# Fourier mixing and SoLU on one core: the first pair's x in 112 rows, F behind the first chunk, four more unread products

## The chip, the cores and the metric

The kernel runs on one core of one Trainium2 chip. The metric is the device time of one execution in microseconds. An execution of a kernel of this size differs from the next by some tenths of a microsecond. PE is TensorE (PEld its weight loads), DVE is VectorE, ACT is ScalarE, POOL is GpSimd and SP is SyncE, which here only issues transfers. TensorE's clock is granted in shares of its full speed.

## The reference

```python
X = np.fft.fft(x, axis=1)           # x: 8 x 3136 x 256, along the sequence
X = np.fft.fft(X, axis=2).real      # along the 256 features
x = X.reshape(25088, 256)
h = x @ w_in                        # w_in: 256 x 1024
e = np.exp(h - h.max(-1)); sm = e / e.sum(-1)
solu = h * sm
ln = (solu - mean(solu)) / sqrt(var(solu) + 1e-6) * g_ln
out = ln @ w_out                    # w_out: 1024 x 256
```

## The kernel before, in words

**Tiling.** The eight sequences are taken in four pairs. A sequence of 3136 is 49 x 64, so a pair has 2 x 49 = 98 rows (`PR`) of 64 positions with 256 features each. `load` (L119) brings a pair in eight chunks of four positions: `xa`, rows of 4 KB each, by a transfer that SP issues (L128), and the mirrored positions `xb` by an indirect transfer that POOL issues (L130, indices in `idx`). Chunk 7 also brings position 0 (L137). For the first pair each of these 16 transfers has 128 rows, though only 98 are used (L133); the 30 others are rows of the next sequence and nobody reads them. For the later pairs they have 98. Chunks 2 to 5 of the first pair land in the buffers called `room`.

**What is done with a chunk.** `add_mirror` (L146, L148) adds the mirrored half on DVE. `fold` (L153, L154, L166) then adds and subtracts the mirrored features into a tile `y`, which has two buffers. `transform1` multiplies with the table `F` on PE: chunks 0 and 2 straight from `xa` with `F` and its negative `minus` (L214), without a fold, the others from `y` (L225). ACT copies the result (L228), and `keep` (L233) stores it to `zd` in the chip's memory. After eight chunks `turn` (L241) reads `zd` back in another order, `transform2` (L253) makes a unit's `q`, and L289 multiplies with the weights: here the steady part begins, 100 units in which PE is nearly always busy. The first unit's first DVE instruction is L302.

**The weights in the opening.** The weights come as 64-bit numbers and are narrowed on DVE and ACT. `w_in` comes in four pieces of 512 KB (L591); piece 0 and 1 make the two halves of `w_in[0]`, 2 and 3 those of `w_in[1]` (`narrow_in`, which ends with L644). The feature transform is put into the weights: `product_in` (L698) multiplies the table `Q` with `w_in`. Its parts are numbered; parts 0 and 2 read `w_in[0]`, parts 1 and 3 read `w_in[1]`. `scale_out` (L722) transposes the gains `gain` on PE, and ACT copies them (L723). `w_out` follows as `raw_out` (L717).

**The order is written by hand.** Nothing is reordered: each engine takes its instructions in the order of the program. For PE in the opening that is: eight unread products (`busy`, L703, with a zeroed table as the operand, which depend on nothing but that table), parts 0 and 2 of `product_in` for two halves of `Wi`, `scale_out`, part 1 for both halves, then `transform1` chunk by chunk, with part 3 after chunks 0 and 3. For DVE: narrowing of the four pieces, with `add_mirror` of chunk 0 between the steps of the last one, then chunk after chunk. For SP: the pieces of `w_in` with `idx` and `Q` among them, `F`, `gain`, then `xa` of chunks 0 to 5; chunks 6 and 7 follow when chunks 0 and 1 are done. Transfers that SP issues use eight semaphores in turn, so the ninth waits until the first has landed, and so on.

Of the kernel before, what the change touches and what calls it, by code (L numbers as in the profile page):

```python
# [17 lines left out]
P = 128  # L18
# [5 lines left out]
PR = 2 * N1  # L24
# [21 lines left out]
def kernel(  # L46
# [19 lines left out]
    nc = tc.nc  # L66
# [23 lines left out]
    F = const.tile([PR, 6, ZR], FP32, name="F")  # L90

    T = [const.tile([P, 2, n, N2], FP32, name=f"T{n}") for n in (KG, NK - KG)]
# [4 lines left out]
    ident = const.tile([P, P], FP32, name="ident")  # L97
# [9 lines left out]
    def result(i):  # L107

        return banks[i % 4]
# [9 lines left out]
    def load(pr, c, room=None):  # L119

        r = slice(pr.p * PR, (pr.p + 1) * PR)
        rows = PR if pr.p else P
        if room is None:
            xa = xpool.tile([P, CH, D], FP32, tag="xa", name="xa")
            xb = xpool.tile([P, CH, D], FP32, tag="xb", name="xb")
        else:
            xa, xb = (t.rearrange("p (l d) -> p l d", d=D) for t in room)
        nc.sync.dma_start(out=xa[0:rows], in_=x_pn[r.start : r.start + rows, c * CH + 1 : (c + 1) * CH + 1, :])  # L128
        i = pr.p * NC + c
        nc.gpsimd.indirect_dma_start(  # L130
            out=xb[0:rows].rearrange("p l d -> p (l d)"), out_offset=None, in_=x_g,
            in_offset=bass.IndirectOffsetOnAxis(ap=idx[0:rows, i : i + 1], axis=0))
        xa, xb = xa[0:PR], xb[0:PR]  # L133
        x0 = None
        if c == NC - 1:
            x0 = xpool.tile([PR, 1, D], FP32, tag="x0", name="x0", bufs=1)
            nc.sync.dma_start(out=x0, in_=x_pn[r, 0:1, :])  # L137
        pr.raw[c] = (xa, xb, x0)
# [441 lines left out]
    NW = 512  # L580
# [66 lines left out]
    class Weights:  # L647
# [50 lines left out]
                nc.tensor.matmul(ps[:, fs], lhsT, self.w_in[c][:, fs], start=(c == 0), stop=(c == KD - 1))  # L698
            return ps

        def busy(self, i, n):
            for _ in range(n):
                nc.tensor.matmul(result(i)[:, 0 : NW // 2], ident, T[0].rearrange("p b k n -> p (b k n)")[:, 0 : NW // 2], start=True, stop=True)  # L703

        def keep_in(self, h, ps):
            nc.scalar.copy(w_mid if h == KD else Wi[:, h, :], ps)
# [62 lines left out]
    def ahead(pr, i, work, after=None):  # L769

        for c in range(NC):
            a = i - SUMS[pr.p][c]
            if work == "load" and (i == (pr.p - 1) * NK and c < 2 and (c or pr.p == 1) or a == 2 and c + 2 < NC):
                load(pr, c if a != 2 else c + 2)
            if work == "mirror" and a in (0, 1):
                behind(add_mirror(pr, c, nc.gpsimd, a), after or units[i - 1])
            if work == "fold" and a in (1, 2):
                fold_part(pr, c, a - 1)
# [24 lines left out]
    with tc.manual_schedule():  # L803
        pairs = [Pair(p) for p in range(NP)]
        first, weights = pairs[0], Weights()
# [13 lines left out]
        weights.piece_in(2)  # L819
        weights.load_tables()  # L820
        weights.piece_in(3)
        nc.sync.dma_start(out=F, in_=f_tab)
        weights.load_gain()
        for c in range(6):
            load(first, c, rooms.get(c))
        nc.vector.memset(ones, 1.0)
        nc.vector.memset(neg_half, -0.5)
        bits(top_bit, neg_half[:, 0:1].bitcast(I32), 31, ALU.logical_shift_right, 31, ALU.logical_shift_left)
# [10 lines left out]
        weights.mid()  # L839
        first.minus = fpool.tile([P, D], FP32, tag="ot1", name="minus", bufs=3)[0:PR, 0:ZR]  # L840
        nc.scalar.mul(out=first.minus, in_=F[:, 1, :], mul=-1.0)
        weights.busy(3, 8)
        made = [weights.product_in(h, (0, 2)) for h in range(KD)]
        weights.scale_out()
        for h in range(KD):
# [1 line left out]
        for c in range(NC):  # L847

            if c:
                add_mirror(first, c, nc.vector)  # L850
            if c not in BY_PE:
                fold(first, c)
            if c == NC - 1:
                for i in range(2):
                    weights.exponent_out(i)
                confine(weights.units[0], True)
                weights.narrow_out(0)
            if c == 3:
                weights.place_out()
                for i in range(2):  # L860
                    weights.load_out(i)
                weights.load_table(0)
            for s in range(CH // 2):
                if c == NC - 1:
                    confine(weights.units[0], parts=(s,))
                transform1(first, c * CH // 2 + s)
            first.raw.pop(c, None)
            if c + 6 < NC:
                load(first, c + 6)
            if c in (0, 3):  # L870
                weights.keep_in(c // 3, weights.product_in(c // 3, (3,), made[c // 3]))
# [310 lines left out]
```

## Time and profile before

| | |
|---|---|
| three executions | 1117.06, 1117.39 (median), 1117.9 us |
| the profiled execution's own time | 1116.79 us |
| its span | 1115.0 us, 22065 instructions |
| granted TensorE clock, mean over the span | 0.998 |
| DMA, mean | 168 GB/s, 187.76 MB |
| DMA in the first fortieth of the span | 338 GB/s, nine tenths busy or more |
| xa and room transfers of the first pair | 512 KB each, 4 + 4 |

How to read it: the span runs from the first to the last instruction of the profiled execution; the 1.8 us between it and the execution's own time lie before and after it. Times of instructions below count from the span's start. In a timeline a row gives start, length, engine, line, operation, output and inputs, shape and how often; brackets give the time for which the engine stood idle just before, and what ended it. Every fp32 matmul has two records, and every packet of a transfer of x is one row of 4096 bytes. A transfer is spread over up to 16 DMA engines, and each engine that takes part posts a share of its semaphore when its own rows have landed; the trace has the time of every such share.

### The profile page before, as it was taken

To read this page: it belongs to the slowest core of one execution; us is meant where nothing else is said; L and a number is where in the kernel's file an instruction comes from. 1 tells how busy PE (TensorE), PEld (TensorE's weight loads), DVE (VectorE), ACT (ScalarE), POOL (GpSimd) and SP (SyncE) were. 2 spreads that over 40 slices of the span, in tenths; PEclk is the share of its full clock that TensorE was granted. 3 is DMA by queue.
4 is the path that set the end of the run, shared out by engine and by line. 5 is a ranking of instruction groups with operands and counts; after the bars stand their busy time and mean duration, and the time that the engine had idled before them with its cause. 6 is when DMAs were issued, how large, how long until landed. Compare 5 with 4: busy or idle time off the path is not lost. (4 is left out here: it accounts for less than half of the span.)

```text
span 1115.0 us, 22065 instructions
## 1 busy us (share of the span) xinstructions
PE 1098.1 (98%) x7063; PEld 877.4 (79%) x7063; DVE 976.0 (88%) x1432; ACT 798.3 (72%) x1947; POOL 808.6 (73%) x709
## 2 busy tenths in 40 slices
PE   8899999999999999999999999999999999999998
PEld 5558787888887878788788778787887788778888
DVE  7998889898888988989889989898898898998884
ACT  5598777777767777777767777777776777777772
POOL 4168888867876979766878878885775676766665
PEclk9999999999999999999999999999999999999999
DMA  9655987757968979765898888776696785865665
GB/s 338 216 175 135 185 206 176 175 135 152 193 155 180 200 181 198 177 151 130 157 176 176 194 185 197 183 174 150 139 163 141 142 169 113 163 141 114 141 132 129
DMA packets 457930, 187.76 MB, mean 168 GB/s; under 512 B 424646, under 2 KB 439254, under 8 KB 457816
## 3 DMA queue, kind: packets, MB, share of 16 engines
q1 hardware_dynamic: 443800, 146.94, 62.1%
q0 software_dynamic: 14016, 39.40, 12.9%
q8 instruction: 58, 0.95, 0.4%
q14 instruction: 56, 0.46, 0.1%
HBM read 46.75 MB, written 38.80 MB: 77 GB/s over the span
## 5 line engine op out<-in xcount | busy, mean ns | idle before, releaser
L289 PE MATMUL ps_h<-Wi,q 128*128 128x512 f32 x800 | 361.6, 593 | 0.4 <-DVE nmax L310 0.2
L465 POOL TENSOR_TENSOR S<-uT 128x512 f32<-128x512 f32 x186 | 237.3, 1276 | 110.9 <-DVE u L325 35.9
L472 PE MATMUL ps_m<-Ws,S 128*128 128x128 f32 x2304 | 296.0, 275 | 0.0
L472 PEld LDWEIGHTS ps_m<-Ws,S 128*128 128x128 f32 x2304 | 279.5, 192 | 3.2 <-issue 0.2
L332 ACT ACTIVATE h<-u,usum 128x1024 f32<-128x1024 f32 x196 | 225.0, 1148 | 73.5 <-DVE u L325 67.3
L289 PEld LDWEIGHTS ps_h<-Wi,q 128*128 128x128 f32 x800 | 144.2, 190 | 144.9 <-issue 141.9
L325 DVE SCALAR_TENSOR_TENSOR u<-h,u 128x1024 f32<-128x1024 f32 x196 | 234.9, 1234 | 10.9 <-ACT u L318 10.8
L318 ACT ACTIVATE u<-h,nmax 128x1024 f32<-128x1024 f32 x196 | 223.3, 1141 | 2.4 <-DVE nmax L310 1.1
L396 DVE STREAM_TRANSPOSE v<-u 128x2048 f32<-128x2048 f32 x88 | 203.4, 2311 | 3.1
L472 PE MATMUL ps_m<-Wo,uT 128*128 128x128 f32 x1536 | 203.7, 276 | 0.0
L472 PEld LDWEIGHTS ps_m<-Wo,uT 128*128 128x128 f32 x1536 | 187.9, 192 | 1.0 <-issue 1.0
L310 DVE CUSTOM_DVE_ANT_0 h<-ev,ps_h 128x1024 f32<-128x1024 f32 x100 | 122.1, 1221 | 17.0 <-DVE ev L302 9.1
L310 DVE CUSTOM_DVE_ANT_0 h<-h,ps_h 128x1024 f32<-128x1024 f32 x96 | 117.2, 1221 | 14.2 <-ACT ot L516 0.5
L559 POOL DMA_INDIRECT out_dram<-ot,idx x96 | 109.0, 1135 | 27.0 <-issue 11.9
L465 POOL TENSOR_TENSOR S<-uT,S 128x512 f32<-128x512 f32 x93 | 118.8, 1277 | 7.2
L465 POOL TENSOR_TENSOR S<-S,uT 128x512 f32<-128x512 f32 x93 | 118.6, 1276 | 7.3
L302 DVE SCALAR_TENSOR_TENSOR ev<-w_mid,r,ps_h 128x1024 f32<-128x1024 f32 x99 | 122.8, 1241 | 0.3
L472 PE MATMUL ps_m<-Ws,uT 128*128 128x128 f32 x768 | 101.8, 276 | 0.0
L472 PE MATMUL ps_m<-Wo,S 128*128 128x128 f32 x768 | 101.4, 275 | 0.0
L253 PEld LDWEIGHTS ps_m<-T,g 128*128 128x128 f32 x400 | 60.0, 191 | 48.1 <-issue 45.9
L507 ACT ACTIVATE ot<-ps_m,rs 128x256 f32<-128x256 f32 x96 | 45.4, 473 | 71.0 <-PE ps_m L472 50.7
L472 PEld LDWEIGHTS ps_m<-Ws,uT 128*128 128x128 f32 x768 | 93.8, 192 | 0.0
(122 smaller groups left out, 1218.1 us busy)
## 6 DMA issues: line engine op xcount, KB each, us to landing
uT<-v SPq DMA_DIRECT2D x752, 128.0 KB
g<-zd POOLq DMA_DIRECT2D x72, 160.0 KB, 4.5
out_dram<-ot SPq DMA_DIRECT2D x176, 64.0 KB
zd<-z SPq DMA_DIRECT2D x24, 400.0 KB
xa<-in_x_dram SPq DMA_DIRECT2D x24, 392.0 KB
raw_in<-in_moe_w_in_dram SPq DMA_DIRECT2D x4, 512.0 KB
xa<-in_x_dram SPq DMA_DIRECT2D x4, 512.0 KB
room<-in_x_dram SPq DMA_DIRECT2D x4, 512.0 KB
```

Of the source, the lines that this page charges most:

```text
L253: nc.tensor.matmul(o, g[:, k, h * P : (h + 1) * P], table, start=(h == 0), stop=True, skip_group_check=True)
L289: nc.tensor.matmul(ps[:, fs], t.q[:, c * P : (c + 1) * P], Wi[:, c, fs], start=True, stop=not whole_even)
L302: nc.vector.scalar_tensor_tensor(out=t.ev, in0=w_mid, scalar=t.r, in1=ps, op0=ALU.mult, op1=ALU.add)
L310: nc.vector.tensor_tensor_reduce(out=t.h[s], in0=t.h[0] if s else t.ev, in1=t.odd, scale=1.0 if s else -0.5, scalar=3.0e38, op0=ALU.add, o ...
L318: nc.scalar.activation(out=t.u[s], in_=t.h[s], func=ACT.Exp, bias=t.nmax[:, s : s + 1], scale=-1.0, accum_out=t.esum[:, s : s + 1])
L325: t.last = nc.vector.scalar_tensor_tensor(out=t.u[s], in0=t.h[s], scalar=-1.0, in1=t.u[s], op0=ALU.mult, op1=ALU.mult, accum_out=t.usum[:, ...
L332: nc.scalar.activation(out=t.h[s], in_=t.u[s], func=ACT.Square, bias=t.usum[:, s : s + 1], scale=-float(FF), accum_out=t.ssq[:, s : s + 1])
L396: nc.vector.transpose(out=t.batch.v[:, :, t.w], in_=t.both.rearrange("p s (g n) -> p (s g) n", n=32))
L465: i = engine.tensor_tensor(out=S[j], in0=a, in1=b, op=op)
L472: nc.tensor.matmul(o, a[:, c], b[:, c], start=start and c == 0, stop=c == n - 1, skip_group_check=True)
L507: nc.scalar.mul(out=self.t.ot[1], in_=self.PP, mul=self.rs[1])
L559: dma = nc.gpsimd.indirect_dma_start(out=out, out_offset=bass.IndirectOffsetOnAxis(ap=idx[:, i : i + 1], axis=0), in_=t.ot[s], in_offset=None)
```

## The change

The 16 transfers of the first pair's x get 112 rows instead of 128. `F` and `gain` are issued after `xa` of chunk 0 instead of before it. `busy` gets its operand as an argument, and after the eight products on the zeroed table four more stand on the first 256 columns of `w_in[0]`; like the eight they write a bank that nobody reads. No other instruction is added or taken away, on no engine, and the order on the others stays.

```diff
@@ load
-        rows = PR if pr.p else P
+        rows = PR if pr.p else 112
@@ Weights
-        def busy(self, i, n):
+        def busy(self, i, n, rhs):
             for _ in range(n):
-                nc.tensor.matmul(result(i)[:, 0 : NW // 2], ident, T[0].rearrange("p b k n -> p (b k n)")[:, 0 : NW // 2], start=True, stop=True)
+                nc.tensor.matmul(result(i)[:, 0 : NW // 2], ident, rhs[:, 0 : NW // 2], start=True, stop=True)
@@ the opening
         weights.load_tables()
         weights.piece_in(3)
-        nc.sync.dma_start(out=F, in_=f_tab)
-        weights.load_gain()
         for c in range(6):
             load(first, c, rooms.get(c))
+            if c == 0:
+                nc.sync.dma_start(out=F, in_=f_tab)
+                weights.load_gain()
...
         nc.scalar.mul(out=first.minus, in_=F[:, 1, :], mul=-1.0)
-        weights.busy(3, 8)
+        weights.busy(3, 8, T[0].rearrange("p b k n -> p (b k n)"))
+        weights.busy(3, 4, weights.w_in[0])
         made = [weights.product_in(h, (0, 2)) for h in range(KD)]
         weights.scale_out()
         for h in range(KD):
             weights.product_in(h, (1,), made[h])
```

With this, SP's order is: the pieces with `idx` and `Q`, `xa` of chunk 0, `F`, `gain`, `xa` of chunk 1 and on. `gain` is now the ninth transfer and takes the wait for the first; `xa` of chunk 0 and `F` wait for none. On PE the first of the four new products waits for DVE's half of `w_in[0]`, and the first product on `Q` for `Q` alone.

## The prediction

> **What bounds the kernel now.** I read the page first: TensorE is busy in nearly the whole span, so a gain in the opening reaches the end only by starting the steady part earlier.
>
> ```profile
> PE 1098.1 (98%) x7063; PEld 877.4 (79%) x7063; DVE 976.0 (88%) x1432; ACT 798.3 (72%) x1947; POOL 808.6 (73%) x709
> ```
>
> The change touches the first 50 us alone. So I went to the table of stretches there (from:to, length, busy time and records of PE, PEld, DVE, ACT and POOL, granted clock, DMA share, GB/s).
>
> ```profile
> 8.22:11.63 3.41, 1.01 (x3) 0.52 (x4) 3.34 (x7) 2.49 (x5) 2.80 (x3) 1.00 1.03 344
> 11.63:15.04 3.41, 3.41 (x6) 1.35 (x5) 3.31 (x7) 2.73 (x5) 2.78 (x3) 0.50 1.02 352
> 18.00:32.20 14.20, 14.08 (x61) 9.98 (x60) 12.85 (x25) 7.11 (x12) 2.39 (x2) 1.00 1.03 410
> 22.00:32.00 10.00, 10.00 (x44) 7.01 (x42) 8.69 (x17) 6.35 (x10) 0.12 (x1) 1.00 1.02 411
> ```
>
> Two things bind from 18 to 32 us: the DMA engines are full at 410 GB/s, and PE has almost no gap. PE ran at half clock from 11.63 to 15.04, after a stretch with 1.01 of 3.41 us busy. Next the DVE timeline, whose brackets name the waits:
>
> ```profile
> 14.58 0.69 DVE L635 SCALAR_TENSOR_TENSOR raw_in<-raw_in,S 128x512 f32<-128x512 uint32 x1
> 16.77 1.22 DVE L146 TENSOR_TENSOR xa<-xa,xb 98x1020 f32<-98x1020 f32 x1 [1.50 <-DMA xa<-in_x_dram]
> ...
> 24.45 1.22 DVE L146 TENSOR_TENSOR room<-room 98x1020 f32<-98x1020 f32 x1 [1.26 <-DMA room<-in_x_dram]
> ...
> 32.86 1.22 DVE L146 TENSOR_TENSOR xa<-xa,xb 98x1020 f32<-98x1020 f32 x1 [0.58 <-DMA xa<-in_x_dram]
> ...
> 38.27 0.75 DVE L594 TENSOR_SCALAR S<-raw_out 128x512 int32<-128x512 int32 x2
> ```
>
> DVE waits for data three times, at chunks 0, 3 and 6, 3.34 us in all. From 32.86 on it works without a pause worth naming until L302 at 50.32, the first unit's start. This is the chain that sets when the steady part begins. PE's timeline shows the products that the change wants warm:
>
> ```profile
> 6.68 0.38 PE L703 MATMUL ps_m<-T,ident 128*128 128x256 f32 x1
> 10.62 5.37 PE L698 MATMUL wps<-w_in,Q 128*128 128x512 f32 x8 [3.56 <-DMA Q<-in_q_tab_dram]
> 15.92 0.22 PE L722 MATMUL ps_m<-ident,gain 8*128 8x8 f32 x1
> 16.07 1.98 PE L698 MATMUL wps<-w_in,Q 128*128 128x512 f32 x4
> 18.12 1.54 PE L214 MATMUL ps_m<-xa,F 98*100 98x258 f32 x6
> ```
>
> And SyncE's queue gives the order in which the transfers stand:
>
> ```profile
> 3.60 0.47 SPq L822 DMA_DIRECT2D F<-in_f_tab_dram  x1
> 4.12 0.27 SPq L678 DMA_DIRECT2D gain<-in_moe_g_ln_dram  x1
> 4.44 1.57 SPq L128 DMA_DIRECT2D xa<-in_x_dram  x2
> ```
>
> **Part 1, 112 rows.** From 14 to 32 us the trace's 4096-byte packets take 159 to 164 ns, and 16 x 4096 B / 159 ns = 412 GB/s, the rate of the table. Each engine alternates between SP's xa and POOL's xb; a chunk is 8 + 8 packets, 16 x 0.16 = 2.56 us, and the last shares of xa for chunks 1, 2 and 3 posted at 19.24, 21.80 and 24.36, 2.56 apart. Every x transfer posts 16 shares, F (98 rows) 14 and gain (8 rows) 8, so I take 112 rows as 16 shares of 7. That makes a chunk 14 x 0.16 = 2.24 us, 0.32 less, and chunk c lands (c + 1) x 0.32 earlier: chunk 3 by 1.28, chunk 6 by 2.24, if a packet keeps its 159 ns.
>
> [...]
>
> **Part 2, F behind chunk 0.** F (98 x 2400 B, 0.10 us a packet) stood before xa of chunk 0. The last shares of the fourth w_in piece, F, gain and xa posted at 12.37, 13.76, 14.11 and 16.67. An engine with F has its w_in share by about 11.7 (second latest of 16; which engine is which the trace does not say); with F gone its xa comes 14 x 0.16 = 2.24 later, 13.9. The latest engine, 12.37, gets there by 14.8. The last share of xb was at 15.38 and has 7 packets, not 8. So chunk 0 is there at about 15.1, and DVE, free at 15.27, starts 1.50 earlier. That lead is not kept: F now stands before chunk 1, whose bytes up to then shrank by two steps only. At chunk 1 DVE would come at 17.87 and xa lands at 19.24 - 0.64 = 18.60, so the lead falls to about 0.67; at chunk 3 it comes at 22.52 and the data at 23.17, lead 1.28. From there chunks 4, 5 and 6 land before DVE wants them (25.3, 27.5 and 30.6 against 25.7, 28.3 and 31.0), the old wait of 0.58 is gone, and the **lead is 1.28 + 0.58 = 1.86 us**. Chunk 7 and the first half of raw_out (last share 37.77, then about 35.2) are in time for DVE at 36.4.
>
> The move's other side: F lands about 13.9 + 7 x 0.26 = 15.7, and gain, 0.35 behind it, at 16.1 instead of 14.11. On SP gain now waits for the first w_in piece (landed 4.34), which costs nothing. On ACT the minus copy (15.58 before) waits for F; behind it stand g_ln and the first z copy at 20.12, so that is hidden. On PE the transpose of gain (L722) stands before four records of product (1,) and all of transform1. They start at about 16.1 + 0.15 instead of 16.07, so transform1 begins **about 0.25 us later**, 18.35. Every later matmul of the opening is queued behind it.
>
> **Part 3, four more products.** Eight records of 128x256. Eleven of L703 in 4.8 to 8.22 took 2.26 us, 0.21 each: 1.7 us, from 8.57 (first half of w_in[0] done) to about 10.3, all beside the wait of 3.56 us for Q. If they ran at half clock they would end at 12.0 and hold the products up by 1.4. They fill the gap that came before the half clock; then the products' eight records take 0.43 instead of 0.85 (spacing of their weight loads) and end at 14.05 instead of 15.9. Nothing is bought with it: w_in[1] is there at 14.21 and gain not before 16.1. The wait for gain is what is late next.
>
> **The sum.** PE, 0.25 late and without gaps, meets DVE at the y buffers, of which there are two: chunk 5's fold (30.91 before) needs chunk 3's products (ended 29.56). With 30.91 - 1.28 = 29.63 against 29.81, DVE loses 0.2. Chunk 6 (32.5 against chunk 4's 32.4) and 7 (34.9 against 34.6) lose nothing. 1.86 - 0.2 = **1.65 us** stays. From 38 to 50 us both ways to the first unit, DVE's work on w_out and z to zd to g to L253, start from DVE's last folds and move as they do; after it nothing changes. The profiled execution took 1116.79 (span 1115.0): 1115.15. It lies 0.6 below the median of 1117.39, so I say **1115.7 us**.
>
> **Bounds of what the trace does not show.** A 112-row load: its packets at 159 ns at best; nearest on the other side are the 98-row loads later in the kernel, whose median packet is 159 in five of the nine that I measured and 201 to 225 ns in four. Where one ran with little beside it, the 14 engines came near their 361 GB/s (14 x 4096 B / 159 ns):
>
> ```profile
> 92.80:93.20 0.40, 0.40 (x6) 0.40 (x5) 0.40 (x3) 0.35 (x1) 0.40 (x1) 1.00 0.94 369
> ```
>
> Five of nine stand at 159, and so do the opening's own packets: I take 159. The best end is that all three waits go: 3.34 us, 1114.1.
>
> **Rivals.**
> 1. Slower: rows that no longer match the engines as 128 did cost more per packet. At 0.205 us a transfer takes 7 x 0.205 = 1.44 instead of 1.27, and 14 transfers up to chunk 6 put it 2.3 us later; DVE waits there already, so the end moves by as much: 1119.7. It decides from 0.182 us a packet on (7 x 0.182 = 8 x 0.159). For it: packets of 190 to 260 ns from 10 to 13.25 us, while F and x ran together. Against it: at 9.25 to 9.75 F's packets ran at their 0.10 with 4096-byte ones at 159 beside them.
> 2. No gain: the bytes shrink, yet a transfer takes as long (0.18 us a packet). Then chunks 3 and 6 land as before: 1117.4.
> 3. The clock drops a second time: PE stands idle from 14.05 to 16.1. That leaves at least 1.4 of any 3.41 us busy; 1.01 led to half clock, 2.26 (4.8 to 8.22) did not, and 1.4 lies between. The price is 1.7 us of PE inside transform1; chunk 5's fold then waits until 31.5 and the lead is eaten: about 1117.2.
>
> **How the numbers follow.** A measurement of this kernel can tell about 0.2%, 2.2 us, from no change. Forecast 0.52 (1114.6 to 1116.4; 0.14 of it under 1115.16, where packets also speed up in the first 13 us), rival 1 0.23, rival 2 0.14, rival 3 0.11. The range leaves out the worst of rival 1 and the last of the best end: 1114.4 to 1119.7. Faster 0.16, same 0.61 (most of the forecast, rivals 2 and 3, a little of rival 1), slower 0.23.
>
> **What would show it.** Right: a spacing of 2.24 us between chunks; DVE's waits at chunk 0 and 6 gone, small ones at 1 and 3; L722 waiting for gain near 16; no half clock after 5 us. Wrong: packets above 0.18 us, L594 (38.27) not earlier, half clock in transform1, or gain before 15 us, which would let PE lead too.

## The result, and the profile after

The changed kernel takes **1126.74 us** (median of four executions, 1125.96 to 1127.95) against 1117.22 for the kernel before in the same comparison (four, 1115.71 to 1117.9): ratio 1.0089, 95% interval 1.0077 to 1.0102. It is slower, by 9.5 us; the prediction was 1115.7 with a range up to 1119.7. The profiled execution took 1127.26 us, with a span of 1125.5.

The page of the kernel after: PE is still busy in 98% of the span. The end came later, the bound stayed.

```profile
PE 1104.8 (98%) x7071; PEld 882.2 (78%) x7071; DVE 975.0 (87%) x1432; ACT 798.9 (71%) x1947; POOL 805.7 (72%) x709
```

The stretches of the kernel after, in the columns of the table of before (stretch, length, PE, PEld, DVE, ACT, POOL, granted clock, DMA share, GB/s):

```profile
14.38:17.79 3.41, 0.07 (x1) 0.00 (x0) 2.17 (x4) 1.85 (x4) 0.00 (x0) 1.00 1.02 251
18.00:32.20 14.20, 12.60 (x42) 8.06 (x43) 7.40 (x14) 3.97 (x8) 2.34 (x2) 0.77 1.04 258
22.00:32.00 10.00, 10.00 (x38) 6.58 (x38) 5.48 (x10) 3.31 (x6) 1.16 (x1) 0.87 1.03 256
41.68:48.51 6.83, 6.31 (x16) 3.94 (x15) 6.70 (x19) 2.52 (x5) 0.00 (x0) 0.50 0.89 309
```

Read the last two columns of the second row together: the DMA engines are as full as before (1.04 against 1.03), but they move 258 GB/s, not 410. Fewer bytes take longer. A full engine at a lower rate means longer packets, and the trace has them: the 4096-byte packets from 18 to 32 us have a median of 261 ns, where they had 160. The granted clock says the second thing: PE, which waits now, runs at half speed in two places (17.79 to 24.61 and 41.68 to 48.51, granted 0.50 in both; 1.00 there before).

DVE's timeline of the kernel after, with what each start waited for in brackets:

```profile
17.07 1.22 DVE L146 TENSOR_TENSOR xa<-xa,xb 98x1020 f32<-98x1020 f32 x1 [1.20 <-DMA xb<-in_x_dram,idx]
...
23.33 1.22 DVE L146 TENSOR_TENSOR xa<-xa,xb 98x1020 f32<-98x1020 f32 x1 [3.58 <-DMA xa<-in_x_dram]
...
26.99 1.22 DVE L146 TENSOR_TENSOR room<-room 98x1020 f32<-98x1020 f32 x1 [0.94 <-DMA room<-in_x_dram]
...
30.53 1.22 DVE L146 TENSOR_TENSOR room<-room 98x1020 f32<-98x1020 f32 x1 [2.25 <-DMA room<-in_x_dram]
...
41.16 1.22 DVE L146 TENSOR_TENSOR xa<-xa,xb 98x1020 f32<-98x1020 f32 x1 [0.59 <-DMA xa<-in_x_dram]
...
46.57 0.75 DVE L594 TENSOR_SCALAR S<-raw_out 128x512 int32<-128x512 int32 x2
...
60.00 1.28 DVE L302 SCALAR_TENSOR_TENSOR ev<-w_mid,r,ps_h 128x1024 f32<-128x1024 f32 x1 [0.72 <-PE ps_h L289]
```

From chunk 1 (23.33) to chunk 6 (41.16) the chunks start some 3.6 us apart, and each of the chunks 0 to 6 waits for its x. L594 starts at 46.57 where it was 38.27: **8.30 us late**. L302, the start of the steady part, is at 60.00 and was at 50.32: **9.68 late**. The row of before, and PE's last products of `transform1` before it:

```profile
38.03 2.40 PE L225 MATMUL ps_m<-y,F 98*100 98x258 f32 x16 [0.39 <-DVE y L166]
...
50.32 1.28 DVE L302 SCALAR_TENSOR_TENSOR ev<-w_mid,r,ps_h 128x1024 f32<-128x1024 f32 x1
```

From L302 to the end of the span it is 1065.5 us after and 1064.7 before; this distance lies between 1064.4 and 1066.1 in all the profiled executions of whole kernels that follow, so no loss can be told from the scatter there. The loss has a large term, late x, and a term of 1.4 us between L594 and L302.

PE's timeline of the kernel after:

```profile
8.46 1.99 PE L703 MATMUL ps_m<-w_in,ident 128*128 128x256 f32 x8
10.76 3.70 PE L698 MATMUL wps<-w_in,Q 128*128 128x512 f32 x8 [0.30 <-DMA Q<-in_q_tab_dram]
19.61 0.27 PE L722 MATMUL ps_m<-ident,gain 8*128 8x8 f32 x1 [5.15 <-DMA gain<-in_moe_g_ln_dram]
19.80 3.78 PE L698 MATMUL wps<-w_in,Q 128*128 128x512 f32 x4
...
44.01 6.34 PE L225 MATMUL ps_m<-y,F 98*100 98x258 f32 x24 [0.52 <-DVE y L166]
```

The four new products did what they were to do: the eight records of `product_in` behind them take 3.70 us, not 5.37. Then PE waits 5.15 us for `gain`, which now stands behind chunk 0 and shares slow DMA engines, and comes back at half clock. The last row is where the 1.4 us are lost: the last products of `transform1` run at half clock and end 3.78 us after the start of L594, where they ended 2.16 after it before.

### The profile page after: what moved, and what is told of

It is laid out like the page before. It is cut to its first block, busy times and chain, and to the rows that moved or that the text cites. A ratio compares the mean times of both kernels' runs of the same rounds, so it can differ in the third digit from the quotient of the medians.

```text
span 1125.5 us, 22080 instructions
## 1 busy us (share of the span) xinstructions
PE 1104.8 (98%) x7071; PEld 882.2 (78%) x7071; DVE 975.0 (87%) x1432; ACT 798.9 (71%) x1947; POOL 805.7 (72%) x709
## 5 line engine op out<-in xcount | busy, mean ns | idle before, releaser
L302 DVE SCALAR_TENSOR_TENSOR ev<-w_mid,r,ps_h 128x1024 f32<-128x1024 f32 x99 | 122.8, 1241 | 0.9 <-PE ps_h L289 0.7
```

Of the source, the lines that this page charges most:

```text
L302: nc.vector.scalar_tensor_tensor(out=t.ev, in0=w_mid, scalar=t.r, in1=ps, op0=ALU.mult, op1=ALU.add)
```

## The experiments

Theory A: rows that are not 128 make every packet of x longer, and this is nearly the whole loss; the author's guess at the cause was that transfers hold each other up where their rows are written. Rival B: the new order (F and gain behind chunk 0) or the new products cost it. Within A, three rivals: the reading side is slow (A2), each 112-row transfer pays a fixed extra of its own (A3), or only the count of rows per engine matters (A4).

**1. The rows alone** (the kernel before with one line changed).

```diff
-        rows = PR if pr.p else P
+        rows = PR if pr.p else 112
```

> The kernel before with one edit, 112 rows for the first pair's x. Theory A (a 112-row transfer runs slower per packet than one of 128 rows): the packets of x take 0.25 to 0.30 us here too, chunks land 3.6 us apart instead of 2.56, and the kernel is 8 to 10 us slower than before, nearly all of the loss. Theory B (the order of F and gain, or the new products, is what slowed the loads down): packets of 0.16 us, chunks 2.24 apart, and about 1.7 us faster than before.

Measured: 1125.54 us (four executions) against 1116.86, ratio 1.0076 (1.0061 to 1.0092). The stretch from 18 to 32.2 us of this kernel:

```profile
18.00:32.20 14.20, 12.34 (x40) 8.75 (x41) 9.29 (x16) 3.85 (x6) 2.34 (x2) 0.76 1.03 261
```

The same 260 GB/s, packets of 253 ns, L594 at 46.20 (the profiled execution is the slowest of the four, 1128.61 us). The rows alone make 8.7 of the 9.5 us; the other 0.8 is less than the two intervals leave open.

**2. The order and the products, without the rows** (the kernel after with this line put back).

```diff
-        rows = PR if pr.p else 112
+        rows = PR if pr.p else P
```

> The changed kernel with its rows put back to 128. Theory A: chunks land 2.56 us apart again; the time is within 1 us of before, since chunks 3 and 6 land when they did and gain, late behind F, costs PE what the warm products save. Theory B: most of the loss stays, 8 us or more.

Measured: 1117.06 (11 executions) against 1116.86 (15), ratio 1.0000 (0.9991 to 1.0009). Rival B falls. DVE and PE of this kernel, from two timelines:

```profile
15.55 1.22 DVE L146 TENSOR_TENSOR xa<-xa,xb 98x1020 f32<-98x1020 f32 x1 [0.32 <-DMA xb<-in_x_dram,idx]
...
19.05 1.22 DVE L146 TENSOR_TENSOR xa<-xa,xb 98x1020 f32<-98x1020 f32 x1 [0.81 <-DMA xa<-in_x_dram]
...
24.17 1.22 DVE L146 TENSOR_TENSOR room<-room 98x1020 f32<-98x1020 f32 x1 [1.25 <-DMA room<-in_x_dram]
```

```profile
16.45 0.22 PE L722 MATMUL ps_m<-ident,gain 8*128 8x8 f32 x1 [2.18 <-DMA gain<-in_moe_g_ln_dram]
16.61 1.99 PE L698 MATMUL wps<-w_in,Q 128*128 128x512 f32 x4
18.43 1.46 PE L214 MATMUL ps_m<-xa,F 98*100 98x258 f32 x6
```

Chunk 0 starts 1.22 us earlier than before (15.55 against 16.77), and of the lead 0.28 is left at chunk 3 (24.17 against 24.45), where the data sets the pace. L594 is at 38.00, L302 at 50.25 (50.32 before).

**3. Loads alone.** Only the loads of x are left, shape after shape.

```diff
+        for load, rows in ((apart, 128), (apart, 112), (joined, 128), (joined, 112), (apart, 98), (apart, 96), (apart, 64), (apart, 120)):
+            for c in range(NC):
+                load(c, rows)
+            landed((one,), rows)
```

> Loads alone, everything else left out: in turn eight transfers each of 128 and 112 rows of x as the kernel takes them (4 KB per row, rows 64 KB apart), 128 and 112 rows that lie one behind the other in memory, then 98, 96, 64 and 120 rows of x, then POOL's gathers of 128 and 112 rows, then both queues together with 128 and with 112. Theory A1 (the slow side is where the rows are written: with 128 rows each engine has a group of rows to itself, with another number several engines meet on one): 128 rows run near 410 GB/s; 112 near 255, whether the source lies apart or joined; both queues together near 255 too. Theory A2 (the slow side is where the rows are read: seven rows per engine at 64 KB steps meet in memory): 112 rows apart near 255, 112 joined near 400. Neither (only something of the whole kernel slows them): all near 400. [...]

Measured. GpSimd's gathers, which wait only for their indices, ran beside the first two shapes, so these are not read. The next shapes ran by themselves; the columns are stretch, length, DVE, POOL, clock, DMA share, GB/s, and the rows are rows lying one behind the other in memory, 128 and then 112 of them, and rows of 98 apart:

```profile
41.00:51.00 10.00, 0.00 (x0) 0.00 (x0) 1.00 1.00 393
55.00:67.00 12.00, 0.00 (x0) 0.00 (x0) 1.00 1.03 280
72.00:81.00 9.00, 0.00 (x0) 0.00 (x0) 1.00 0.90 304
```

96 rows gave 274 GB/s, 64 rows 214, 120 rows 228. Packets: 159 ns for 128 rows, 238 for 112, 193 for 98, 249 for 96, 328 for 64, 277 for 120. Of these shapes only 128 rows, at 393 GB/s, come near the 410 of the kernel before. With both queues loading 112 rows (185 to 203 us) it was 254 GB/s, as in the kernel.

**4. 112 rows from contiguous memory** in the whole kernel, so that only the writing side is as in the change (the first pair works on other data).

```diff
-        rows = PR if pr.p else P
+        rows = PR if pr.p else 112
...
-        nc.sync.dma_start(out=xa[0:rows], in_=x_pn[r.start : r.start + rows, c * CH + 1 : (c + 1) * CH + 1, :])
+        nc.sync.dma_start(out=xa[0:rows].rearrange("p l d -> p (l d)") if pr.p == 0 else xa[0:rows], in_=x_g[c * P : c * P + rows] if pr.p == 0 else x_pn[...])
...
-    mirror[PR:, :NC] = np.arange(PR, P)[:, None] * (N2 // CH) + N2 // CH - 1 - np.arange(NC)
+    mirror[:, :NC] = 2048 + np.arange(P)[:, None] + P * np.arange(NC)
```

> As e1_rows_alone, but the first pair's x is read from rows that lie one behind the other in memory, by SP and by POOL: other data of the same size, so the first pair's part of the output is that of other inputs. Theory A1 (writing side): packets of 0.25 to 0.30 us and chunks 3.6 us apart stay, 1125 to 1127 us. Theory A2 (reading side): packets of 0.16 us, chunks 2.24 us apart, about 1115.5 us.

Measured: 1128.15 us (one execution), 260 GB/s from 18 to 32.2 us, packets of 252 to 259 ns, L594 at 47.57. A2 falls: rows that lie one behind the other in memory are loaded as slowly as rows 64 KB apart.

**5. Where the rows are written**, again with loads of x alone, on one queue.

```diff
+        for place, rows in ((first(128), first(128)), (first(112), first(112)), (first(64), first(64)), (lambda t: t[64:128], first(64)), (first(48), first(48)), (first(32), first(32)), (first(16), first(16)), (lambda t: t[0:128:8], first(16)), (first(128), first(128))):
+            for c in range(NC):
+                load(c, place, rows)
+            landed()
```

> All of the kernel's work is left out: only loads of x remain, eight transfers of one shape after another on SyncE's queue, and a copy that waits for each shape. [...] Theory 2 (a transfer that is not of 128 rows pays one fixed extra per packet, wherever its rows lie): 260 ns for every shape but 128, and the two of 16 rows alike. Theory 3 (fewer successive rows per engine, less collision): packets get shorter from 112 rows to 16.

Measured, median packets: 128 rows 159 ns, 112 rows 235, 64 rows 320 on the lower and 319 on the upper half, 48 rows some **440**, 32 rows 322. The rows for 112, 64 (lower half) and 48, in the columns of the last table:

```profile
18.00:30.00 12.00, 0.00 (x0) 0.00 (x0) 1.00 1.03 284
34.00:44.00 10.00, 0.00 (x0) 0.00 (x0) 1.00 0.97 204
...
62.00:71.00 9.00, 0.00 (x0) 0.00 (x0) 1.00 0.92 132
```

A fixed extra falls (it would be 235 to 260 everywhere), and so does A4: 48 rows have the longest packets, and in experiment 3 the same count of rows per engine has different ones. There 112 and 98 rows posted 16 and 14 shares, seven rows each, and took 238 and 193 ns; 128 and 120 rows posted 16 and 15, eight rows each, and took 159 and 277. Sixteen rows gave 233 ns, and 215 when spread over every eighth partition: their transfers are so short that the engines were busy only 46% and 33% of the time (131 and 92 GB/s), so they could overlap little, and this pair decides nothing. Why a shape has the packets it has was not shown: that engines hold each other up where they write stays the author's guess, and no trace here shows which engine writes what.

**6. 112 rows on one queue alone.** The sharpest test between A and A3: under A the 112-row transfers of SP must also slow the 128-row gathers of POOL.

```diff
+        some = PR if pr.p else 112
-        nc.sync.dma_start(out=xa[0:rows], in_=x_pn[r.start : r.start + rows, ...
+        nc.sync.dma_start(out=xa[0:some], in_=x_pn[r.start : r.start + some, ...
```

> The kernel before with 112 rows only in SyncE's x transfers of the first pair; GpSimd's gathers keep 128 rows. [...] Theory 2 (a fixed extra on each packet of a 112-row transfer): 7 x 0.26 + 8 x 0.16 = 3.1 us a chunk against 2.56, +0.54 a chunk, near 1121 us, and GpSimd's packets stay at 160 ns.

Measured: 1125.17 us, one execution. POOL's packets, unchanged in number and shape, took 236 ns, like SP's.

```profile
18.00:32.20 14.20, 11.03 (x46) 7.12 (x45) 9.33 (x16) 4.53 (x7) 2.39 (x2) 1.00 1.03 282
```

Half of the change costs nearly all of it, and a transfer of good shape pays for the one beside it. A3 falls. So slow packets of one queue held up those of the other (236 ns against 159 before). That they meet on the way into SBUF was the author's guess; it fits experiment 4, where reading from other places left the packets at 252 to 259 ns, but no run shows the place.

**7. 98 rows, only what is used.**

```diff
-        rows = PR if pr.p else P
+        rows = PR
```

> The kernel before with 98 rows in the first pair's x, the rows that are used, on 14 engines with 7 rows each. In the run of loads alone a packet of 98 rows took 191 ns, so a transfer is 7 x 0.191 = 1.34 us against 8 x 0.159 = 1.27 for 128 rows: 0.13 us more per chunk of two transfers, about 0.9 us over the seven chunks that pace the opening, near 1118 us (1117 to 1120). If every transfer that is not of 128 rows costs what 112 rows cost, 1125 to 1127. If only the bytes counted, 7 x 0.159 = 1.11 us a transfer and under 1117.

Measured: 1125.39 against 1116.65, ratio 1.0080 (1.0063 to 1.0097). My 1118 was wrong: I took 191 ns from a run with one queue. With two full queues the packets took 280 ns:

```profile
18.00:32.20 14.20, 11.84 (x46) 7.17 (x45) 7.67 (x12) 4.46 (x7) 2.37 (x2) 1.00 0.97 220
```

The 30 rows that nobody reads pay for themselves.

**8. to 10. The parts of the order.** F and gain moved, without the products; the products alone; both, with gain left ahead of chunk 0.

```diff
@@ 8 and 10: the move (in 10 without load_gain)
-        nc.sync.dma_start(out=F, in_=f_tab)
-        weights.load_gain()
...
+            if c == 0:
+                nc.sync.dma_start(out=F, in_=f_tab)
+                weights.load_gain()
@@ 9 and 10: the products
+        weights.busy(3, 4, weights.w_in[0])
```

> The kernel before with only F and the gain moved behind chunk 0 (128 rows, no further products). As the prediction's second part has it: DVE starts chunk 0 earlier by 1.2 to 1.5 us, waits for x in chunks 1, 3 and 6 and loses it again, and the gain comes some 0.3 us too late for the last products on w_in: no change, 1117 us, within 0.2%. Rival: the lead is kept, 1115.6 us.

> The kernel before with only the four further unread products on w_in (128 rows, F and gain ahead of chunk 0). They take 1.7 us of TensorE beside its wait for Q and keep its clock from halving at 11.6 us (3.4 us at half clock before): products on w_in end some 1.5 us earlier. The first transform waits for chunk 0 anyway: no change, 1117 us, within 0.2%. Rival: the earlier end counts, 1116 us.

> The kernel after with 128 rows and with the gain left ahead of chunk 0; only F goes behind it. The products on w_in no longer wait for the gain, so the first transform can start with chunk 0, near 17 us instead of 18.4. Since DVE waits for x later on (chunks 1, 3 and 6), the last chunk still ends when its x lands: no change, 1117 us. Rival: the late gain is what cost the order its gain, 1115.7 us.

Measured, each from 11 executions against 27 of before (1116.94): 1116.76, ratio 1.0003 (0.9994 to 1.0012); 1116.43, 0.9997 (0.9988 to 1.0006); 1116.98, 1.0001 (0.9991 to 1.0010). None changes the time. In the third, gain is in time and transform1 starts at 17.26 instead of 18.43, but L302 is at 50.26 all the same. No version here beats the kernel before.

**11. to 13. The clock's share.** Unread products after chunks 4, 5 and 6 of the kernel after (11); the kernel after again (12), and beside it on the same chip products after chunks 4 and 5 alone (13).

```diff
             first.raw.pop(c, None)
+            if c in (4, 5, 6):
+                weights.busy(2 * c + 2, 4, weights.w_in[0])
```

> The kernel after, with four more unread products behind each of chunks 4, 5 and 6 of the first pair (12 products, 24 records), in the time in which TensorE waits for x. Theory (the loss has two terms: 8.3 us of late x, and 1.4 us more because the waiting TensorE drops to half clock from 41.7 to 48.5 us and the last chunks' products run at it): the half clock behind 41 us goes, the chunk paces and the landing of the last x stay, the first activation input (line 302) moves from 60.0 to 58.5 us or a little before, and the time from 1126.7 to about 1125.3 us. Rival (all 9.7 us follow from the late x alone): 1126.7, unchanged, or later by products in the way.

> The kernel after, once more, so that the next kernel can be set beside it on one chip: about 1126.7 us, 1.0089 of before.

> The kernel after with four unread products behind chunks 4 and 5 only. If the half clock at 41.7 us costs time of its own: no half clock behind 41 us, line 594 to line 302 takes 12.05 to 12.3 us as in the kernels without it (13.4 in the kernel after), and the time is 1.1 to 1.4 us below that of the kernel after on this chip. If all of the loss follows from late x alone: the same time as the kernel after, and the distance from line 594 to line 302 stays at 13 us.

Measured: 11: 1124.97, ratio to before 1.0083 (1.0066 to 1.0100). 12: 1126.44, 1.0086 (1.0072 to 1.0100). 13: 1124.31, 1.0069 (1.0055 to 1.0083). In 11 and 13 the half clock behind 41 us is gone.

```profile
34.85:38.26 3.41, 3.41 (x17) 2.83 (x16) 2.33 (x5) 1.18 (x3) 0.00 (x0) 1.00 1.03 265
38.27:41.68 3.41, 3.25 (x16) 2.36 (x14) 2.67 (x5) 1.17 (x2) 0.00 (x0) 1.00 1.04 277
...
43.39:46.80 3.41, 2.23 (x16) 1.81 (x15) 3.38 (x11) 1.51 (x4) 0.00 (x0) 1.00 0.95 318
```

These are three stretches of 13; in the first trace of the kernel after the second of them had 1.55 us of PE. The median of 13 is 2.1 us below that of 12. But the profiles don't let me give this to the clock: L594 came at 45.09 in 13 and at 47.59 in 12, since x's packets took 251 against 271 ns, in part long before the first added product; and 13 has no half clock near 18 us either, which the products cannot have caused. What the traces do show is the distance from L594 to L302: 11.88 to 12.26 us in seven executions without half clock in it (before, 2, 7, 8, 9, 10, 13), and 12.44 to 14.47 in the five with it (after 13.43, and 1, 4, 6, 12). Experiment 11, without it, took 12.78, with four products in the way of chunk 7. The last products of `transform1` show how: they end 2.1 to 2.2 us after L594 starts in the seven, and 3.0 to 4.9 after it in four of the five. In the fifth, experiment 4, the half clock comes later (55.84 to 59.25) and falls on the way from these products to L302, which takes 12.1 us there and 9.3 to 10.1 in all the others. So executions with half clock there lose **0.4 to 2.4 us** against the 12.1 of the seven, differently in each; how much of the median this makes stays open.

## Why the prediction was wrong

**Part 1 failed, at the step "if a packet keeps its 159 ns".** It took 261 ns; the split into 16 shares was as assumed. By the prediction's own arithmetic a transfer is then 7 x 0.261 = 1.83 us instead of 1.27, and the 14 transfers up to chunk 6 make 7.8 us; chunk 6 (41.16 against 32.86) and L594 came 8.3 late. The direction of rival 1 was right, and so was its point of decision (0.182 us); its price of 0.205 was too low, so that it stopped at 1119.7, and the range with it. The choice rested on five of nine 98-row loads, and on one stretch of 0.4 us, where such loads met little traffic. Experiment 7 shows what the same loads do beside a second full queue: 280 ns. The four loads at 201 to 225 ns, which I counted as the minority, were the ones to follow, and the trace of before tells them from the others. Of the 22 transfers of 98 rows that SP issues for xa from 90 us on, the 17 that had at most 44 of POOL's 4096-byte packets beside them have a median packet of 159 ns (one of them 194); the five that had 57 to 94 beside them have 201 to 252. In the opening both queues load side by side all the time, so the upper end had to lie above these. The packets of 190 to 260 ns beside F, which rival 1 had on its side, were another sign: F has 98 rows too. What makes the packets of such rows longer no run shows.

**Part 2 held, apart from the rows.** Experiment 2 has chunk 0 at 15.55 where 15.27 was expected, a wait at chunk 1 (0.81), and 0.28 us of the lead left at chunk 3. The prediction had 1.28 left there, all of it from shorter transfers; they did not come, and it went. PE had gain at 16.45 (16.1 expected, and 0.15 to its use), and transform1 at 18.43 (18.35).

**Part 3 held in its end, not in its detail.** In experiment 2 the new records took 0.25 us each, 2.0 in all (0.21 and 1.7 expected), and were done at 10.6, about when Q was there; the products (0, 2) ended at 14.3 (14.05 expected). Nothing was bought, as forecast.

**The sum** of 1.65 us therefore lost its only lasting term, the earlier landing of chunks 3 and 6.

**Rival 3**, a second drop of the clock in the wait for gain, came true in the kernel after (17.79 to 24.61), for another reason: PE waited 5.15 us, not 2.05. In experiment 2, with a wait of 2.18, the clock stayed up. What that drop costs by itself was not tried; DVE has chunk 1 only at 23.33 in any case.

**What would show it** was right in its list: packets above 0.18 us, L594 not earlier, and half clock in transform1 are what the trace has.

## What to carry to other kernels

A transfer's price depended on its shape and on what else filled the DMA engines (98 rows: 193 ns a packet on one queue alone, 280 beside a second full one), so take it from rows with the same traffic beside them; a packet's time in a quiet stretch was only a lower end (159 ns). Cutting rows of a load to save bytes can lower the rate by more than the bytes: here 128 rows, 30 of them unread, beat both 112 and 98 (410 GB/s from 18 to 32.2 us against 261 and 220, and 1117 us against 1125.5 and 1125.4). In a stretch that is bound by DMA, moving a transfer gave back later what it gained first: chunk 0 started 1.22, 1.20 and 0.86 us earlier in experiments 2, 8 and 10, and at chunk 3 a lead of 0.28 was left in 2, and none in 8 and 10.

## What the runs showed of the hardware

- The rate by rows was not monotonic, with 4096-byte packets on one queue (experiments 3 and 5; the DMA engines 0.88 to 1.03 busy): 128 rows 413 GB/s, 112 rows 284, 98 rows 304, 96 rows 274, 120 rows 228, 64 rows 204, 32 rows 204, 48 rows 132.
- One queue with a bad shape slowed the other: POOL's 128-row packets went from 159 to 236 ns beside 112-row ones (experiment 6).
- PE's clock changed on a grid of 3.41 us in these openings: every half-clock stretch lasted one, two or three times that (11.63 to 15.04 before, 17.79 to 24.61 after, 40.24 to 50.48 in experiment 1). In the openings of thirteen profiled executions, all thirteen full-clock stretches with 0.07 to 1.55 us of busy PE were followed by half clock, and none with 1.88 us or more; of five between (1.59 to 1.83) three were. The 1.4 that the prediction left between "yes" and "no" was a yes.
